# Four row tiles of the seventh sequence in the input's buffers, its routing drawn together, and the first experts' work half a step earlier

## The chip, the core and the metric

The kernel runs on one core of one Trainium2 chip. The core has five engines that run their own instruction streams and meet at semaphores: TensorE (PE), VectorE (DVE), ScalarE (ACT), GpSimd (POOL) and SyncE (SP), which issues most of the DMA transfers. The metric is the device time of one execution in microseconds (us).

## What is computed

The input is 8 sequences of 2496 rows of 256 numbers. Each is filtered in the frequency domain, and its 19968 result rows go through a mixture of 8 experts, one expert for each row.

```python
X = np.fft.rfft(x, axis=1)                      # x: 8 x 2496 x 256
y = np.fft.irfft(X * (filt_r + 1j * filt_i), n=2496, axis=1)
x = y.reshape(19968, 256)
logits = x @ w_gate                             # 8 experts
expert_idx = np.argmax(logits, axis=1)
gate_w = softmax(logits)[expert_idx]            # of each row
for e in range(8):
    xe = x[expert_idx == e]
    out[expert_idx == e] = gate_w * (np.maximum(xe @ w1[e], 0) @ w2[e])   # 256 -> 1024 -> 256
```

## The kernel before

**Tiling.** The transform of length 2496 is taken as 39 x 64 in two stages of matmuls. A unit u is one sequence b and one half h of the 256 columns, so there are 16 units. The middle of the transform is cut into 80 steps t, five to a unit. A step runs through the engines so: `spec1` transposes on PE (`pt`) and copies on ACT (`z`, line 317); `spec2` multiplies on PE (`px`); `filt_` makes three products with the filter on DVE (`tr`, `ti`, `ti`, lines 345 to 347); `join` adds them (`p`, line 355: POOL for the steps below 71, DVE after that); `spec3` multiplies back on PE (`pi`) and ACT copies the result to memory (`U`, line 371). Below, px77 is the `px` of step 77. The input of a unit comes in tiles `x` from a pool `xp` with 4 buffers under the tag "x" (`loadx`), and `forward1` reads them (`f`).

**A sequence's tail.** When both units of a sequence are in `U`, its routing chain begins, `route1` to `route6`: products with the gate (`plw`, `lw`, `pgl`, `gl`, `pl`), the choice of the expert (`rmx`, `lg`, `eq`, `oh`), ranks inside each expert's block by a product with a triangle (`pp`) and a scan (`sa`, `sb`), and the number of the slot that each row goes to (`dest`, line 623). Beside it the inverse runs over 11 row tiles j of two row groups each: `inv1` transposes (`pg`) and copies on ACT (`gh`, line 639), `inv2` multiplies (`py`) and copies on ACT into a row tile `yt` (line 649; 5 buffers), `inv3` adds the gate's value and the row's number to `yt` (DVE, line 656) and scatters the two row groups to the table `xs` in DRAM by an indirect DMA that POOL issues (line 158): 22 scatters for a sequence.

**The experts.** `weights` closes the pools that the transform no longer needs, the input's `xp` among them, and opens the experts' in the same memory. A block is 128 rows of one expert. `load` reads it (`xb`, line 957, on SP's queue), `loadw` brings an expert's weights in two transfers of about 1 MB (`wa` and `wb`, line 991, SP). `prep` (DVE, lines 1009 to 1018) finds a power-of-two scale, `split` writes the rows as two halves in f16 (`xs`, ACT line 1023 and DVE line 1024), `turn` transposes them by a DMA (`xt`, line 1031, SP). `layer1` (`ph`), the halves `hs`, `hh`, `hl`, `layer2` (`po`) and `out_` (`ot`) follow. The first blocks of the experts hold rows of the first six sequences only, so they can run before the last two are done.

**What sets the order.** No scheduler: each piece is given a number by `at(key, f, ...)`, the pieces are sorted by it and written out, and every engine works through its own instructions in that order, waiting at the head of its queue. The unit of the key is one step; `PLACE[0]` = 80.9 is the key at which the first expert block runs. `RT` holds the places of the ten parts of a routing chain, times a factor `c`.

Of the kernel before, what the change touches and what calls it, by code (L numbers as in the profile page):

```python
# [9 lines left out]
F32 = mybir.dt.float32  # L10
# [17 lines left out]
GP = 3 * N1  # L28
DUP = 18
NPAIR = NG // 2  # L30
ROW = 260
NW = 2
# [81 lines left out]
def tile_fft_moe(ctx, tc, x, filt_r, filt_i, w_gate, w1, w2, cst, out):  # L114
    nc = tc.nc
    B = x.shape[0]
# [9 lines left out]
    for b, m in ((B - 3, 8), (B - 1, 20)):  # L126
        sure = -(-(S * (b + 1) - E * 127) // 128)
        n = min(m, -(-(sure - taken - E) // 2))
# [56 lines left out]
    with ExitStack() as fctx:  # L185
# [5 lines left out]
        wp = pool(name="wp", bufs=2)  # L191
# [8 lines left out]
        xp = early(name="xp", bufs=4)  # L200
# [33 lines left out]
        def loadx(u, c, eng=(nc.sync,) * 3):  # L234
            b, h = divmod(u, 2)
            xv = x[b].rearrange("(n1 n2) d -> n1 n2 d", n2=N2)[
                :, :, h * 128 : (h + 1) * 128
            ]
            g0, g1 = (HEAD if u < 2 else BANKS)[c]
            if u < 2 and c < 2:  # L240
                t = Uf[2 + u][:GP, 128 * g0 : 128 * g1]
                t = t.rearrange("p (g d) -> p g d", d=128)
            else:
                t = xp.tile([GP, 4, 128], F32, name=f"x{u}_{c}", tag="x")
            for l in range(3):
                n = min(g1, NG if l == 0 else NG - 1) - g0
                s0 = 3 * g0 + l
                eng[l].dma_start(
                    t[l * N1 : (l + 1) * N1, :n, :],
                    xv[:, s0 : s0 + 3 * (n - 1) + 1 : 3, :],  # L250
                )
            for g in range(g0, g1):
                xt[u, g] = t[:, g - g0, :]
# [388 lines left out]
        def inv2(b, j):  # L642
            gh = sti.pop((b, j))
            ps = (pY if b < B - 1 else pB).tile(
                [128, 2, D], F32, name=f"py{b}_{j}", tag="pY" if b < B - 1 else "pF"
            )
            nc.tensor.matmul(ps[:GP], lhsT=dm, rhs=gh[:GP], start=True, stop=True)  # L647
            yt = wp.tile([GP, 2, ROW], F32, name=f"yt{b}_{j}", tag="yt", bufs=5)
            nc.scalar.copy(yt[:, :, :D], ps[:GP])
            sti[b, j] = yt  # L650

# [102 lines left out]
        for c in range(3):  # L754
            loadx(0, c)
# [11 lines left out]
        for j in range(6):  # L767
            forward1(0, j)
        loadx(1, 0)
        loadk(bm, "bm", 1, 2)  # L770
        loadf(1, 2)
        loadx(1, 1)
        loadx(1, 2)
        twice(0)
# [29 lines left out]
        def at(key, f, *a):  # L804
            work.append((key, f, a))
# [18 lines left out]
        K = {"s2": 1.394, "sr": 1.65, "si": 1.85, "s3": 3.6, "f": 0.063, "fd": 0.75, "w": 6.0, "wp": 4.1}  # L824
        RT = (0.0, 0.4, 0.45, 0.9, 1.3, 1.7, 2.2, 2.5, 2.9, 3.3)
        slow = lambda t: min(1.0, max(0.6, 1.0 - 0.06 * (t - 72)))
        for t in range(NT):
            u, it = divmod(t, 5)
# [9 lines left out]
            if 0 < u and u + 1 < NU_ALL and it == 0:  # L838
                for j in range(6):

                    n = 6 * (u + 1) + j - 4
# [10 lines left out]
        PLACE = (80.9, 90.5, 110.5)  # L852
        done = []
        for b in range(B):
            rho = slow(10 * b + 9)
            s0 = 10 * b + 9 + K["s3"] * rho + 0.05
            c = 1.0 if b < B - 1 else 0.6
            for i, f in enumerate(
                (
                    (route1, 0),  # L860
                    (route1b, 0),
                    (route1, 1),
                    (route1b, 1),
                    (route2,),
                    (route3,),
                    (route4,),
                    (route4b,),
                    (route5,),
                    (route6,),
                )  # L870
            ):
                at(s0 + c * RT[i], f[0], b, *f[1:])
            lead = 2.0 if b < B - 1 else 1.3


            t = 10 * b + 20
            d = 0.55
            if b < B - 1:
                z = PLACE[0] - 2.75 if b == B - 2 else t + K["s3"] * slow(t) - 0.15
                d = min(0.75, (z - s0 - lead) / (NPAIR - 1))  # L880
            for j in range(NPAIR):
                z = s0 + lead + j * d
                at(z, inv1, b, j)
                at(z + 0.7 * c, inv2, b, j)
                z = max(z + 1.2 * c, s0 + c * RT[9] + 0.1 + 0.9 * d * j)
                for gg in range(2):
                    at(z + 0.45 * d * gg, inv3, b, j, gg)
            if b in [r for r, _, _ in SEG]:
                for s, v in enumerate(SEG):
                    if v[0] == b:  # L890
                        at(s0 + c * RT[9] + 0.2 + 0.1 * s, finish, s)
            done.append(z)
            if b == B - 1:
                at(z + 0.1, tails)
                for e in range(E):
                    at(z + 1.2 + e, tail, e)
        for q in range(2 * E):
            e, i = divmod(q, 2)
            z = K["w"] + K["wp"] * q
# [197 lines left out]
        for s, (r, m, n) in enumerate(SEG):  # L1097
            n *= m
            a = PLACE[s]
            z = PLACE[s + 1] if s + 1 < len(SEG) else a + 0.5 * n  # L1100
# [8 lines left out]
        opened = lambda s: done[SEG[s][0]] + 0.4  # L1109

        def when(k, n):

            s, i, m, b0 = units[k]
            b = b0 + m - 1
            z, d, _ = tau[b]
            if n == 0:
                return z + 0.5 * d
            nx, dx = (tau[b + 1][0], tau[b + 1][1]) if b + 1 < NB else (z + d, d)
            return nx + 0.95 * dx

        at(PLACE[0] - 2.0, weights)
        for k in range(nu):
            s, i, m, b0 = units[k]
            z, d, _ = tau[b0]
            at(max(opened(s), z - 2.0, PLACE[0] - 1.95), load, k)
            for n in range(2):
                at(max(opened(s) + 0.02, when(k - NW, n) + 0.01 if k >= NW else PLACE[0] - 1.9 + 0.7 * (2 * k + n), PLACE[0] - 1.9), loadw, k, n)
        for b in range(NB):
            z, d, s = tau[b]
            y = max(opened(s) + 0.3, z - 1.1)  # L1130
            at(y, prep, b)
            at(y + 0.05, split, b)
            at(y + 0.1, turn, b)
            at(z, layer1, b, 0)
            at(z + 0.2 * d, halves, b, 0)
            at(z + 0.25 * d, layer1, b, 1)
            at(z + 0.45 * d, halves, b, 1)
            nx, dx = (tau[b + 1][0], tau[b + 1][1]) if b + 1 < NB else (z + d, d)
            at(nx + 0.5 * dx, layer2, b, 0)
            at(nx + 0.75 * dx, layer2, b, 1)  # L1140
            at(nx + 0.95 * dx, out_, b)
            at(nx + 0.95 * dx + 0.5, send, b)
# [4 lines left out]
        n = nc.values_load(nblk[0:1, 0:1], min_val=0, max_val=NBLK)  # L1147
# [50 lines left out]
```

## Time and profile before

| | us |
|---|---|
| median of 3 runs | 1410.51 |
| lowest and highest run | 1407.64 and 1411.91 |
| profiled execution, its time | 1408.65 |
| profiled execution, its span | 1406.7 |
| PE busy in the span | 1313.4 (93%) |
| ACT, DVE, POOL busy | 846.1, 834.4, 466.2 |
| mean granted clock of TensorE | 0.988 of full speed |

The span is the time from the first to the last instruction of the profiled execution; 1.95 us lie around it. All times in the text count from the span's start. In a line of the timeline stand the start, the duration, the engine, the line of the code, the operation, what it writes and reads, the number of instructions that were put together, and in brackets how long the engine was idle before it and what released it.

### The profile page before, as it was taken

The numbers are of one execution on the slowest core, as the hardware profiler recorded it, in microseconds if no ns is written. First come the engines' busy times: TensorE is split into PE (matmuls) and PEld (weight loads), VectorE is DVE, ScalarE is ACT, GpSimd is POOL, SyncE is SP. The second block draws the span as 40 slices with busy tenths as digits, with TensorE's granted clock in tenths as the row PEclk, the third lists the DMA queues.
The fourth block names the chain that finished last, engine by engine and source line by source line (L and its number), as shares of the span: only waits on it lengthen the run. The fifth ranks groups of instructions, "written<-read, shape, count | busy, mean of one in ns | idle before, by whom it ended". The sixth has DMA issues, their size and how long they took to land.

```text
span 1406.7 us, 39039 instructions
## 1 busy us (share of the span) xinstructions
PE 1313.4 (93%) x14855; PEld 1175.6 (84%) x14855; DVE 834.4 (59%) x2391; ACT 846.1 (60%) x1444; POOL 466.2 (33%) x446
## 2 busy tenths in 40 slices
PE   6789999989999599899999998999999999999997
PEld 5777777777777477789999987999999999999997
DVE  1688879888796455345555554555555555555552
ACT  3567667766676355455665655665655666666654
POOL 3527476484654513423211111111111111111111
PEclk9999999999999899999999999999999999999999
DMA  9746555564643343496373389337337336336431
GB/s 175 205 139 203 164 190 179 165 194 147 193 129 107 108 114 81 118 272 185 83 192 79 79 240 300 78 74 197 75 75 192 76 77 192 81 76 159 111 74 43
DMA packets 198272, 197.71 MB, mean 141 GB/s; under 512 B 104008, under 2 KB 177339, under 8 KB 189827
## 3 DMA queue, kind: packets, MB, share of 16 engines
q1 hardware_dynamic: 178142, 151.96, 40.0%
q0 software_dynamic: 19472, 42.51, 10.9%
q8 instruction: 118, 1.93, 0.6%
q10 hardware_dynamic: 468, 0.72, 0.2%
q14 instruction: 72, 0.58, 0.1%
HBM read 344.12 MB, written 61.56 MB: 288 GB/s over the span
## 4 chain that ended last, share of the span: by engine, by line
PE 57%; DMA 5%; issue 3%; DVE 2%; ACT 1%; SPq 1%; another core or an unknown queue 1%; POOL 0%; POOLq 0%; ACTq 0%; DVEq 0%
PE ph L1044 27%; PE po L1070 26%; DMA wa<-wscr 3%; PE py L647 1%; PE pg L633 1%; PE px L326 1%; DMA wb<-wscr 1%; DMA xt<-xs 1%; PE pi L366 1%; DMA xs<-yt,dest 0%; POOL out_dram L158 0%; DVE hl L1058 0%; PE f L263 0%; PE plw L497 0%
## 5 line engine op out<-in xcount | busy, mean ns | idle before, releaser
L1044 PE MATMUL ph<-xt,wa 128*128 128x128 f16 x7728 | 463.2, 220 | 18.5 <-DMA wa<-wscr 7.9
L1044 PEld LDWEIGHTS <-wa 128*128 128x128 f16 x7728 | 447.4, 98 | 29.9 <-issue 14.4
L1070 PE MATMUL po<-wb,hh 128*128 128x256 f16 x2576 | 431.2, 273 | 6.1 <-ACT ot L1086 4.3
L1058 DVE TENSOR_TENSOR hl<-hs,hh 128x512 f16<-128x512 f32 x322 | 222.9, 692 | 350.9 <-ACT hh L1052 296.5
L158 POOL DMA_INDIRECT out_dram<-ot,t x161 | 158.2, 982 | 672.8 <-DVE xs L1024 570.2
L1070 PE MATMUL po<-wb,hl 128*128 128x256 f16 x1288 | 351.1, 273 | 0.0
L1070 PEld LDWEIGHTS <-hh 128*128 128x128 f16 x2576 | 245.5, 98 | 36.6 <-issue 8.4
L1050 ACT ACTIVATE hs<-ph 128x512 f32<-128x512 f32 x322 | 191.8, 596 | 104.5 <-PE ph L1044 83.9
L158 POOL DMA_INDIRECT xs<-yt,dest x176 | 185.2, 1052 | 139.5 <-issue 76.3
L1023 ACT ACTIVATE xs<-xb,s 128x256 f16<-128x256 f32 x161 | 82.1, 510 | 226.6 <-DVE s L1013 222.0
L1052 ACT CAST hh<-hs 128x512 f16<-128x512 f32 x322 | 199.5, 620 | 10.3
L1070 PEld LDWEIGHTS <-hl 128*128 128x128 f16 x1288 | 126.1, 98 | 14.8
L371 ACT COPY U<-pi 128x512 f32<-128x512 f32 (+1 forms) x80 | 87.3, 1091 | 59.8 <-PE pi L366 42.2
L355 POOL TENSOR_TENSOR p<-tr,ti 128x512 f32<-128x512 f32 x71 | 91.1, 1283 | 94.6 <-DVE ti L347 79.0
L1024 DVE SCALAR_TENSOR_TENSOR xs<-xb,s,xs 128x256 f16<-128x256 f32 x161 | 78.0, 484 | 59.6 <-ACT xs L1023 58.5
L647 PE MATMUL py<-gh,dm 117*117 117x512 f32 x176 | 93.0, 609 | 12.1 <-issue 9.2
L326 PEld LDWEIGHTS px<-z,bm 128*128 128x128 f32 x640 | 80.9, 195 | 18.7 <-issue 11.4
L366 PE MATMUL pi<-cm,p 128*128 128x128 f32 (+1 forms) x640 | 86.8, 279 | 8.4 <-POOL p L355 6.8
L263 PE MATMUL f<-a,x 117*128 117x117 f32 (+1 forms) x628 | 87.7, 278 | 5.1 <-ACT U L371 1.8
L326 PE MATMUL px<-z,bm 128*128 128x128 f32 x640 | 88.4, 282 | 3.2 <-ACT z L317 1.4
L366 PEld LDWEIGHTS pi<-cm,p 128*128 128x128 f32 x640 | 78.8, 193 | 12.2 <-POOL p L355 7.2
L345 DVE TENSOR_TENSOR tr<-px,ff 128x512 f32<-128x512 f32 x80 | 54.8, 685 | 57.6 <-PE px L326 25.9
(171 smaller groups left out, 1339.6 us busy)
## 6 DMA issues: line engine op xcount, KB each, us to landing
wb<-wscr SPq DMA_DIRECT2D x133, 1040.0 KB
wa<-wscr SPq DMA_DIRECT2D x133, 1024.0 KB
xb<-xs SPq DMA_DIRECT2D x161, 130.0 KB
wf<-in_moe_w_dram SPq DMA_DIRECT2D x32, 512.0 KB
x<-in_x_dram SPq DMA_DIRECT2D x210, 78.0 KB
wscr<-wh SPq DMA_DIRECT2D x8, 1040.0 KB
wscr<-wh SPq DMA_DIRECT2D x8, 1024.0 KB
xs<-yt,dest POOLq DMA_INDIRECT x176
```

The source lines that it names most:

```text
L158: nc.gpsimd.indirect_dma_start(out=dst, out_offset=bass.IndirectOffsetOnAxis(ap=idx, axis=0), in_=src, in_offset=None, bounds_check=bound, ...
L263: nc.tensor.matmul(ps[:, n : n + m], lhsT=xt.pop((u, g))[:m], rhs=a1[:m, :m], start=True, stop=True,)
L326: nc.tensor.matmul(ps[:, kk], lhsT=bm[:, 4 * it + kk], rhs=z[:, kk], start=True, stop=True,)
L355: e.tensor_tensor(p, tr, ti, op=ALU.add)
L366: nc.tensor.matmul(ps[:, o : o + n], lhsT=p[:, kk], rhs=cm[:, k, :n], start=True, stop=True)
L371: nc.scalar.copy(U[u % NU].rearrange("p n r -> p r n")[:, r0 : r0 + o // 64, :], ps[:, :o].rearrange("p (r n) -> p r n", n=N2),)
L647: nc.tensor.matmul(ps[:GP], lhsT=dm, rhs=gh[:GP], start=True, stop=True)
L1044: nc.tensor.matmul(ps[:, f], lhsT=w[:, p : p + 128], rhs=xt[:, r, c], start=(n == 0), stop=(n == 5))
L1050: nc.scalar.activation(s, ps, AF.Relu, scale=1.0 / B23)
L1052: nc.scalar.copy(hh, s)
L1058: nc.vector.tensor_tensor(hl, s, hh, op=ALU.subtract)
L1070: nc.tensor.matmul(ps, lhsT=h2[q][:, f % 4], rhs=wv[:, r, f], start=(f == 0 and n == 0), stop=(f == 7 and n == 2),)
```

## The change

The 7th of the 8 sequences is b = 6, in the code `B - 2`. For it alone:

1. The tiles under the tag "x" get the size of a row tile pair, and row tiles 5 to 8 of the sequence take buffers of that tag, where the input's tiles were, so that its 11 row tiles have 9 buffers in place of 5.
2. Its routing chain's places are multiplied by 0.75 (before 1.0), and the key at which its inverse has to be through is 0.55 of a step earlier.
3. `weights`, the first loads of blocks and weights, and the first block's `prep`, `split` and `turn` stand 0.5 to 0.85 of a step earlier.

```diff
@@ loadx
-                t = xp.tile([GP, 4, 128], F32, name=f"x{u}_{c}", tag="x")
+                t = xp.tile([GP, 2 * ROW], F32, name=f"x{u}_{c}", tag="x")
+                t = t[:, 0:512].rearrange("p (g d) -> p g d", d=128)
@@ inv2
-            yt = wp.tile([GP, 2, ROW], F32, name=f"yt{b}_{j}", tag="yt", bufs=5)
+            if b == B - 2 and j % 9 > 4:
+                yt = xp.tile([GP, 2 * ROW], F32, name=f"yt{b}_{j}", tag="x")
+                yt = yt.rearrange("p (g d) -> p g d", d=ROW)
+            else:
+                yt = wp.tile([GP, 2, ROW], F32, name=f"yt{b}_{j}", tag="yt", bufs=5)
@@ the routing chain's and the inverse's keys
-            c = 1.0 if b < B - 1 else 0.6
+            c = {B - 1: 0.6, B - 2: 0.75}.get(b, 1.0)
-                z = PLACE[0] - 2.75 if b == B - 2 else t + K["s3"] * slow(t) - 0.15
+                z = PLACE[0] - 3.3 if b == B - 2 else t + K["s3"] * slow(t) - 0.15
@@ the experts' keys
-        at(PLACE[0] - 2.0, weights)
+        at(PLACE[0] - 2.5, weights)
-            at(max(opened(s), z - 2.0, PLACE[0] - 1.95), load, k)
+            at(max(opened(s), z - 2.0, PLACE[0] - 2.45), load, k)
...
-            y = max(opened(s) + 0.3, z - 1.1)
+            y = max(opened(s) + 0.3, z - (1.1 if b else 1.95))
```

The line between, for `loadw`, has its two -1.9 replaced by -2.4. The number of instructions is the same on every engine; POOL's order is the same too. The other engines' orders differ only from the routing of the 7th sequence to the first blocks of the experts. (Line numbers of the changed kernel are 1 higher up to line 648 and 5 higher from there.)

On PE, in the routing: `pl` is the logits' product, `pp` the ranks' product, `pt` is of step 74, `px` of 73, `pi` of 71. Before:

```order
L538 MATMUL pl_5055<-gl_4996,dm 117x176
L311 MATMUL pt_5063<-ident,T_110 128x128 x4
L326 MATMUL px_5070<-z_4994,bm 128x128 x4
L366 MATMUL pi_5089<-cm,p_4980 128x128 x4
L633 MATMUL pg_0_5095<-ident,U_122 117x128
...
L574 MATMUL pp_5104<-oh_5077,ltri 117x176
```

After:

```order
L539 MATMUL pl_5041<-gl_4989,dm 117x176
L264 MATMUL f_15_5_5057<-a_112,x_5_4863 128x117
L264 MATMUL f_15_5_5057<-a_112,x_5_4863 128x39
L312 MATMUL pt_5072<-ident,T_110 128x128 x4
...
L575 MATMUL pp_5079<-oh_5065,ltri 117x176
...
L327 MATMUL px_5082<-z_5012,bm 128x128 x4
L367 MATMUL pi_5097<-cm,p_4980 128x128 x4
```

`px`, `pi` and `pg_0` moved from ahead of `pp` to behind it, and the last piece of `f` from ahead of `pl` to between the two.

On PE, from the last but one row tile's product to the first expert matmul `ph`; the `pi` are those of steps 76 to 78 before, and of 75 to 78 after. Before:

```order
L647 MATMUL py_9_5388<-gh_9_5336,dm 117x512
L366 MATMUL pi_5396<-cm,p_5304 128x128 x4
L647 MATMUL py_10_5405<-gh_10_5372,dm 117x512
L326 MATMUL px_5409<-z_5358,bm 128x128 x4
L311 MATMUL pt_5441<-ident,T_111 128x128 x4
L366 MATMUL pi_5476<-cm,p_5379 128x128 x4
L326 MATMUL px_5496<-z_5446,bm 128x128 x4
L366 MATMUL pi_5519<-cm,p_5467 128x128 x4
L1044 LDWEIGHTS wa_5430
L1044 MATMUL ph_0_5549<-xt_5503,wa_5430 128x128
```

After:

```order
L648 MATMUL py_9_5363<-gh_9_5334,dm 117x512
L367 MATMUL pi_5371<-cm,p_5261 128x64
L367 MATMUL pi_5371<-cm,p_5261 128x128 x3
L327 MATMUL px_5377<-z_5293,bm 128x128 x4
L312 MATMUL pt_5382<-ident,T_111 128x128 x4
L648 MATMUL py_10_5392<-gh_10_5354,dm 117x512
L367 MATMUL pi_5444<-cm,p_5340 128x128 x4
L327 MATMUL px_5450<-z_5387,bm 128x128 x4
L312 MATMUL pt_5475<-ident,T_111 128x128 x4
L367 MATMUL pi_5494<-cm,p_5405 128x128 x4
L327 MATMUL px_5500<-z_5480,bm 128x128 x4
L367 MATMUL pi_5526<-cm,p_5491 128x128 x4
```

pi75, px77 and pt78 stood ahead of `py_9` before and stand behind it after, so `py_9` and the row tiles ahead of it moved forward.

On SP, the experts' first transfers, with the reads of table entries between them left out. Before:

```order
L957 DMA xb_5437<-xs 128x260
...
L991 DMA wa_5430<-wscr 128x4096
...
L991 DMA wb_5431<-wscr 128x4160
L1031 DMA_TRANSPOSE xt_5503<-xs_5489 128x4x128
...
L957 DMA xb_5513<-xs 128x260
```

After:

```order
L962 DMA xb_5458<-xs 128x260
...
L1036 DMA_TRANSPOSE xt_5484<-xs_5468 128x4x128
...
L996 DMA wb_5427<-wscr 128x4160
...
L996 DMA wa_5428<-wscr 128x4096
...
L962 DMA xb_5520<-xs 128x260
```

The first `wa` now stands ahead of the first `xb`; the first `wb` and the second expert's `wa` stand behind the first transpose `xt`, and the third and fourth blocks' `xb` behind both.

On DVE the first block's `prep` and its part of `split` stand ahead of the filter blocks of steps 78 and 79 (before: between the two), and `dest` stands two filter blocks behind the choice of the expert's first instruction `rmx` (before also two, and one more between `gl` and `rmx`). On ACT the first block's `xs` stands behind `z` of step 79 and ahead of `U` of steps 77 and 78 (before: behind `U` of step 77).

More of the change, by code (lines that the diff above doesn't have):

```diff
@@ L1124, in tile_fft_moe @@
             z, d, _ = tau[b0]
-            at(max(opened(s), z - 2.0, PLACE[0] - 1.95), load, k)
+            at(max(opened(s), z - 2.0, PLACE[0] - 2.45), load, k)
             for n in range(2):
-                at(max(opened(s) + 0.02, when(k - NW, n) + 0.01 if k >= NW else PLACE[0] - 1.9 + 0.7 * (2 * k + n), PLACE[0] - 1.9), loadw, k, n)
+                at(max(opened(s) + 0.02, when(k - NW, n) + 0.01 if k >= NW else PLACE[0] - 2.4 + 0.7 * (2 * k + n), PLACE[0] - 2.4), loadw, k, n)
         for b in range(NB):
             z, d, s = tau[b]
-            y = max(opened(s) + 0.3, z - 1.1)
+            y = max(opened(s) + 0.3, z - (1.1 if b else 1.95))
             at(y, prep, b)
```

## The prediction

> **What bounds the kernel now.** I read the page first, then the windows, then the timelines of the stretch that the change touches.
>
> ```profile
> span 1406.7 us, 39039 instructions
> PE 57%; DMA 5%; issue 3%; DVE 2%; ACT 1%; SPq 1%; another core or an unknown queue 1%; POOL 0%; POOLq 0%; ACTq 0%; DVEq 0%
> ```
>
> PE carries most of the chain that ends last. What matters is where it is not full. The windows give from, to, length, then the busy time of PE first, and the granted clock, DMA share and GB/s last.
>
> ```profile
> 464.00:468.00 4.00, 4.00 (x26) 2.71 (x24) 0.00 (x0) 1.20 (x3) 3.08 (x4) 1.00 0.34 103
> 472.00:476.00 4.00, 0.00 (x0) 0.00 (x0) 2.44 (x7) 0.84 (x2) 2.32 (x3) 0.57 0.24 78
> 476.00:480.00 4.00, 0.69 (x1) 0.47 (x2) 0.00 (x0) 1.41 (x3) 3.08 (x4) 0.50 0.30 91
> 496.00:500.00 4.00, 2.94 (x35) 2.12 (x36) 1.78 (x3) 2.85 (x5) 0.00 (x0) 0.95 1.12 380
> 500.00:540.00 40.00, 37.20 (x447) 31.48 (x440) 26.18 (x124) 21.01 (x41) 7.12 (x7) 1.00 0.26 68
> 600.00:620.00 20.00, 17.17 (x234) 15.83 (x232) 10.64 (x39) 11.07 (x22) 5.05 (x5) 1.00 0.86 252
> 620.00:640.00 20.00, 20.00 (x269) 18.68 (x267) 10.46 (x35) 12.34 (x23) 6.18 (x6) 1.00 1.09 313
> ```
>
> PE is full up to 468, nearly empty to 480, and full again from 620. So the change works on the one large hole in the middle, the handover from the transform to the experts, and since PE has no slack after 620, a first expert matmul that starts x earlier ends the kernel x earlier, if the last sequence's chain between 500 and 620 moves along. It should: it begins behind that first block. PE on both sides of the hole:
>
> ```profile
> 441.30 0.53 PE L538 MATMUL pl<-gl,dm 117*117 117x176 f32 x2
> 445.81 0.29 PE L574 MATMUL pp<-oh,ltri 117*117 117x176 bf16 x1 [1.32 <-DVE oh L565]
> 465.37 0.60 PE L311 MATMUL pt<-ident,T 128*128 128x128 f32 x4
> 467.15 1.02 PE L647 MATMUL py<-gh,dm 117*117 117x512 f32 x2
> 468.92 1.16 PE L366 MATMUL pi<-cm,p 128*128 128x128 f32 x8 [0.74 <-issue]
> 479.31 2.06 PE L647 MATMUL py<-gh,dm 117*117 117x512 f32 x2 [9.24 <-issue]
> 485.68 1.16 PE L326 MATMUL px<-z,bm 128*128 128x128 f32 x8 [1.36 <-ACT z L317]
> 487.40 1.13 PE L366 MATMUL pi<-cm,p 128*128 128x128 f32 x8 [0.56 <-DVE yt L656]
> 492.58 4.47 PE L1044 MATMUL ph<-xt,wa 128*128 128x128 f16 x48 [4.05 <-DMA xt<-xs]
> 503.55 2.85 PE L1044 MATMUL ph<-xt,wa 128*128 128x128 f16 x48
> ```
>
> PE waits 0.74 + 9.24 + 1.36 + 0.56 + 4.05 = 15.95 us between 468 and 492.58. The 9.24 are py_10's, which needs gh_10. ACT, DVE, POOL and SP say why:
>
> ```profile
> 465.49 0.59 ACT L649 COPY yt<-py 117x512 f32<-117x512 f32 x1 [1.74 <-DMA xs<-yt,dest]
> 473.59 0.59 ACT L317 COPY z<-pt 128x512 f32<-128x512 f32 x1 [4.72 <-remote]
> 475.74 0.59 ACT L649 COPY yt<-py 117x512 f32<-117x512 f32 x1 [1.57 <-remote]
> 478.68 0.59 ACT L639 COPY gh<-pg 117x512 f32<-117x512 f32 x1 [2.35 <-remote]
> 479.16 0.59 ACT L649 COPY yt<-py 117x512 f32<-117x512 f32 x1
> 483.62 1.10 ACT L371 COPY U<-pi 128x512 f32<-128x512 f32 x1 [3.87 <-PE pt L311]
> 488.07 0.51 ACT L1023 ACTIVATE xs<-xb,s 128x256 f16<-128x256 f32 x1 [1.42 <-DVE s L1013]
> 498.24 0.51 ACT L1023 ACTIVATE xs<-xb,s 128x256 f16<-128x256 f32 x1
> 498.65 1.08 ACT L371 COPY U<-pi 128x512 f32<-128x512 f32 x1
> 441.07 0.68 DVE L345 TENSOR_TENSOR tr<-px,ff 128x512 f32<-128x512 f32 x1
> 443.80 0.33 DVE L547 TENSOR_REDUCE rmx<-pl 117x22 f32<-117x176 f32 x1
> 454.34 0.18 DVE L623 TENSOR_TENSOR dest<-df,dup 117x22 int32<-117x22 f32 x1
> 471.45 0.69 DVE L345 TENSOR_TENSOR tr<-px,ff 128x512 f32<-128x512 f32 x1 [8.58 <-PE pi L366]
> 487.17 0.17 DVE L656 COPY yt<-meta 117x8 f32<-117x8 f32 x1
> 455.44 0.99 POOL L158 DMA_INDIRECT xs<-yt,dest  x1 [15.12 <-issue]
> 481.67 0.99 POOL L158 DMA_INDIRECT xs<-yt,dest  x1 [0.30 <-issue]
> 479.08 0.33 SPq L991 DMA_DIRECT2D wb<-wscr  x1
> 489.12 1.31 SPq L1031 DMA_TRANSPOSE xt<-xs  x1
> 491.16 0.90 SPq L957 DMA_DIRECT2D xb<-xs  x2
> ```
>
> The striking thing is z78 at 473.59. Its `pt` began at 465.37 and took 0.60, so its result was there at 465.97, and ACT waited 4.72 us for "remote", a releaser that the profile does not name. The next two results of PE, py_8 and pg_10, were used at 475.74 and 478.68, both long after PE had left them. So in this stretch PE's results are taken up late, one after another, about (478.68 - 471.45) / 3 = 2.41 us apart, while POOL issues scatters back to back. I can't say from the trace why; how much of it remains is the main unknown of this prediction.
>
> **The change part by part.**
>
> *Four more buffers (5 to 9 for 11 row tiles).* Before, yt_5 and later ones waited for the scatters of yt_0 and later. Now only yt_9 and yt_10 reuse a buffer, whose scatters are some ten us older. That takes away ACT's waits like the 1.74 at yt_7 (465.49), which sat under PE's full stretch: nothing by itself. What it adds: the experts' memory now lies over buffers that yt_5 to yt_8 hold until their scatters land. The first tiles behind that wait, `hh` and `hl` of block 0, need yt_7's, the 15th and 16th scatter. At (481.67 - 455.44) / 19 = 1.38 us or less each, the 16th is issued by about 454.4 + 15 x 1.38 = 475.1; with a few us to land that is before the first `ph` of any case below but the quickest. I take 0.
>
> *The routing chain drawn together.* One filter block (443.80 - 441.07 = 2.73 us) leaves the path from `gl` to `rmx`, and `pl` itself comes one `px` and a wait earlier, by my reading at about 439.65. Then `rmx`, `lg`, a block, `eq` to `oh`: `pp` at about 445.0. Before it was 445.81, but PE had done px, pi and pg_0 ahead of it. What these take at PE's full pitch stands in the chain of waits:
>
> ```profile
> 452.80 0.44 PE pg L633 x4
> 453.24 0.89 PE px L326 x8
> ```
>
> A `pi` has the shape of a `px`, a `pt` that of a `pg`, so the three are 0.89 + 0.89 + 0.44 = 2.2 us. So PE's full stretch loses 2.2 - 0.8 = 1.4 us at `pp`: the one cost in this part that nothing covers. `dest` comes some 3 us earlier, at about 451.5, but yt_0's copy of `meta` now stands behind step 74's tr, ti, ti, and I put the first scatter at 454.4 against 455.44, so 1 us earlier. Nothing waits on PE for that. The last of the 22 would be issued at 454.4 + 21 x 1.30 = 481.7.
>
> *Row tiles ahead of pi75, px77, pt78.* py_9 ended at 467.15 + 1.02 = 468.17. Now 1.4 later for `pp`, and 2.2 earlier, since pi75, px77 and pt78 (0.89 + 0.89 + 0.44) stand behind it: 467.4. pt78 then ends at about 469.6 instead of 465.97. What this buys: gh_10 no longer stands behind z78 and yt_8 on ACT, so py_10 doesn't keep PE waiting for two late results.
>
> *Preparation and xs ahead.* Before, from DVE's end of yt_10's copy (487.17, behind p77) to `ph` lay 492.58 - 487.17 = 5.41 us. That tail remains, but it moves ahead of the filter blocks of steps 78 and 79 and, on ACT, right behind z79. It saves the waits for pi77 and U77, which before lay between 483.62 and 488.07 (4.45 us).
>
> *SP's queue.* `xt0` no longer stands behind `wb0`, which waited until 479.08 for the last read of `U`; `xt0` was issued at 489.12, so that wait hid nothing and its removal gives 0. On the other side xb2 and xb3 now queue behind wb0 and wa1, 2.1 MB. At the 380 GB/s of the window from 496, when weights were moving, that is 5.5 us; at the 103 of the window from 464, 20 us. In the likeliest case wb0 goes out at about 482.7, so xb2 lands by 488 to 503, and `xs` of block 2, which stands ahead of U79 on ACT, needs it 498.24 - 492.58 = 5.7 us after `ph` starts, at about 492. The cost is between 0 and 11; the row from 496 is the one with the same transfers in flight, so I take 0 and keep the rest for the range. [...]
>
> *The sum.* Five late results of PE stand on the way from py_9 to the first block's `xs`: px77, pt78, py_10, pi76, pt79 (ACT takes U76 and z79 in order ahead of xs0). I start at the first late one of before, 471.45, and keep the pitch of 2.41: the fifth is taken at 471.45 + 4 x 2.41 = 481.1. z79 takes 0.59, xs0 starts at 481.7, and from xs0 to `ph` it is 492.58 - 488.07 = 4.5: `ph` at 486.2, 6.4 us earlier. Against the profiled execution's 1408.65 that is 1402.3, against the median, which is 1.86 higher, 1404.1. I say 1403.
>
> **The rivals.**
>
> *The lateness goes away (a larger gain).* With results taken up at once, px77 ends at 469.3, DVE's three products, yt_9's copy and p77 end at 472.2, and 5.4 us later `ph` starts: 477.7, 14.9 earlier. Then `ph` also would not run slowly: its first 48 matmuls took 4.47 us where the next 48 took 2.85, so 1.6 more. Less what xb2 may cost, 12 to 16 earlier: 1393 to 1398. For it: the row tiles now leave in a steady stream and ACT's queue has no head that waits for buffers. Against: the scatters are as dense as before. [...]
>
> *The head start is used up (no change).* `ph` starts some 5 us earlier, but xb2's 0 to 11 us hold U79 and with it the last sequence's routing, on which the stretch from 500 to 620 hangs, or that stretch's idle time (2.80 us from 500 to 540, 2.83 from 600 to 620) grows by as much. For it: U79 began at 498.65 directly behind `xs` of block 2 (498.24), so that there is no slack between the two. Against: the 380 GB/s. That gives 1407 to 1412.
>
> *More results late (slower).* The pitch applies not to the five results on the path but to each one in the burst. In the new order pg_10, py_9, pi75 and px78 stand between them in PE's order, all read by ACT or DVE. Nine results from 471.45 on put the last at 471.45 + 8 x 2.41 = 490.7, xs0 at 491.3 and `ph` at 495.8, 3.2 later than before: 1412 to 1414, some us more with xb2. It decides from the eighth result on (xs0 was at 488.07: (488.07 - 0.59 - 471.45) / 2.41 = 6.7 pitches). For it: the same dense scatters, without the pauses of before, so with no place to catch up. Against: yt_9 at 479.16 came 0.48 behind gh_10, so not each result pays.
>
> **How the numbers follow.** A measurement of this kernel tells about 0.3%, 4.2 us, from no change; against the median that means faster below 1406.3 and slower above 1414.7. Forecast, `ph` 4 to 9 us earlier: 0.40, own range 1399 to 1406. Lateness gone, 1393 to 1398: 0.24. Used up: 0.23. More late, or xb2 at its worst, 0.13; about half of it is over 1414.7, and some of the used-up cases go there too. So faster 0.64, same 0.24, slower 0.12. The range leaves out the lowest twentieth and the slower side's end: 1393 to 1412.
>
> **What would show it.** Right: the first `ph` between 483 and 489; z79 and xs0 next to each other on ACT; PE's wait ahead of `pp` about 3 to 4 us instead of 1.32; py_9 ending within 1 us of before; no wait over 1 us for a scatter on `hh` or `hl` of block 0; U79 between 491 and 494; PE full from about 613. Wrong: results of PE taken up at once (then 1395), xs of block 2 waiting for xb2 (then no gain), or ACT waits for "remote" that reach past 488 (then slower).

## The result and the profile after

The changed kernel is slower: 1416.66 us median against 1408.03 for the kernel before on the same chip, a ratio of 1.0054 (95% interval 1.0044 to 1.0065), or 7.6 us. The forecast was 1403, faster. The changed kernel's profiled execution took 1417.81 us, its span was 1415.9.

PE around the handover, from the changed kernel's timeline:

```profile
443.09 0.40 PE L575 MATMUL pp<-oh,ltri 117*117 117x176 bf16 x1 [3.52 <-DVE oh L566]
443.43 1.98 PE L327 MATMUL px<-z,bm 128*128 128x128 f32 x8
445.21 1.92 PE L367 MATMUL pi<-cm,p 128*128 128x128 f32 x8
463.26 1.12 PE L648 MATMUL py<-gh,dm 117*117 117x512 f32 x2 [2.45 <-issue]
475.31 1.03 PE L648 MATMUL py<-gh,dm 117*117 117x512 f32 x2
481.05 0.60 PE L312 MATMUL pt<-ident,T 128*128 128x128 f32 x4
489.47 2.08 PE L327 MATMUL px<-z,bm 128*128 128x128 f32 x8 [6.93 <-ACT z L318]
495.06 4.83 PE L1049 MATMUL ph<-xt,wa 128*128 128x128 f16 x48
503.72 0.80 PE L498 MATMUL plw<-U,wg 128*32 128x351 f32 x8 [2.15 <-ACT U L372]
508.67 3.21 PE L1049 MATMUL ph<-xt,wa 128*128 128x128 f16 x48
```

The first `ph` starts at 495.06 (before 492.58, forecast 486.2). The great wait has not gone but moved: before it was 9.24 us at py_10, now it is 6.93 at px79. A second cost stands at `pp`: PE waits 3.52 us and then runs px and pi at half speed (1.98 and 1.92 us, with a pitch of 1.78 and 1.70, in place of 0.89). The second `ph` has lost more than the first, 508.67 against 503.55. Of the 9.2 us by which the span is longer, 2.5 have built up by the first `ph` and 5.1 by the second; the rest comes later, and no experiment takes it apart.

The other engines there, from the same kernel:

```profile
450.52 0.18 DVE L624 TENSOR_TENSOR dest<-df,dup 117x22 int32<-117x22 f32 x1
471.33 0.69 DVE L346 TENSOR_TENSOR tr<-px,ff 128x512 f32<-128x512 f32 x1 [10.93 <-remote]
488.83 0.59 ACT L318 COPY z<-pt 128x512 f32<-128x512 f32 x1 [5.40 <-remote]
489.32 0.51 ACT L1028 ACTIVATE xs<-xb,s 128x256 f16<-128x256 f32 x1
501.34 0.42 DVE L1014 TENSOR_REDUCE m<-xb 128x1 f32<-128x257 f32 x1 [3.76 <-DMA xb<-xs]
502.58 1.08 ACT L372 COPY U<-pi 128x512 f32<-128x512 f32 x1
453.94 0.99 POOL L158 DMA_INDIRECT xs<-yt,dest  x1 [13.35 <-ACT gh L640]
468.21 1.00 POOL L158 DMA_INDIRECT xs<-yt,dest  x1 [0.30 <-issue]
474.47 0.99 POOL L158 DMA_INDIRECT xs<-yt,dest  x1 [5.26 <-ACT gh L640]
486.12 1.00 POOL L158 DMA_INDIRECT xs<-yt,dest  x1 [0.31 <-issue]
```

Put the POOL rows beside the two "remote" waits. PE's results are late from some 6 us after POOL's first scatter, all are there at 471.3, 2 us after POOL paused (469.2), nothing is late from 474 to 481, and z79, whose `pt` ended at 481.65, is taken at 488.83, 1.7 us after POOL's last scatter ended (487.12). In the kernel before, the same had happened at 483.6, 0.95 us after its sixth scatter of the second run. So in these two traces lateness sets in some 6 us into an unbroken run of scatters, and what is still held when the run ends is let go 1 to 2 us behind it. Some results are let through singly inside a run, as the four of the kernel before between 471.45 and 478.68; what decides that isn't shown.

The same shows further on in the kernel before, where the 8th sequence's scatters and the outputs' make two runs of six, one from 568.78 to 576.43. PE, from the timeline of before:

```profile
573.89 0.44 PE L1044 MATMUL ph<-xt,wa 128*128 128x128 f16 x5
574.75 0.22 PE L1044 MATMUL ph<-xt,wa 128*128 128x128 f16 x1 [0.41 <-issue]
575.47 0.22 PE L1044 MATMUL ph<-xt,wa 128*128 128x128 f16 x1 [0.51 <-issue]
576.22 0.22 PE L1044 MATMUL ph<-xt,wa 128*128 128x128 f16 x1 [0.53 <-issue]
577.63 3.80 PE L1044 MATMUL ph<-xt,wa 128*128 128x128 f16 x40 [1.19 <-issue]
```

From 5.5 us after the run's start PE, waiting for nothing that the profile names, gets out one matmul in about 0.7 us, and it goes on at full pace 1.2 us after the run has ended. So it is not only that its results are seen late.

To compare kernels, lateness is worked out thus: the trace has the moments at which PE's semaphore rises; from each I subtract the end of PE's last finished instruction that raises it, and take the largest difference within a run of scatters and the 1.5 us behind it. A run is unbroken where less than 0.7 us lies between two; the outputs' indirect DMAs count with the scatters.

### The profile page after: what moved, and what is told of

Its sections match the earlier page's. It is cut to its first block, busy times and chain, and to the rows that moved or that the text cites. A ratio compares the mean times of both kernels' runs of the same rounds, so it can differ in the third digit from the quotient of the medians.

```text
span 1415.9 us, 39040 instructions
## 1 busy us (share of the span) xinstructions
PE 1321.5 (93%) x14855; PEld 1181.1 (83%) x14855; DVE 833.4 (59%) x2391; ACT 846.5 (60%) x1444; POOL 465.4 (33%) x446
## 4 chain that ended last, share of the span: by engine, by line
PE 47%; DMA 5%; issue 2%; DVE 1%; SPq 1%; ACT 1%; POOL 0%; POOLq 0%
PE ph L1049 24%; PE po L1075 23%; DMA wa<-wscr 2%; DMA wb<-wscr 2%; DVE hl L1063 0%; POOL out_dram L158 0%; DMA xt<-xs 0%; DMA xb<-xs 0%; SPq L1036 0%; SPq L948 0%; DVE m L1014 0%; ACT hh L1057 0%; ACT hs L1055 0%; ACT xs L1028 0%; DVE xs L1029 0%
```

## The experiments

Theory A: unbroken runs of scatters on GpSimd make PE's results late. Theory B: the data of the scatters, or the order of the work, does. Theory C: the drawn-together routing costs at `pp`. Theory D: the loads behind 2.1 MB of weights cost.

**Pauses in the changed kernel.**

```diff
+        pad = fp.tile([128, 256], F32, name="pad")      # and a memset
...
             scatter(xs[:, :], dest[:, g : g + 1], yt[:, gg], ...)
+            if b == B - 2 and g % 3 == 2:
+                for _ in range(2):
+                    nc.gpsimd.tensor_tensor(pad, pad, pad, op=ALU.mult)
```

> The changed kernel with two small GpSimd multiplies on a scratch tile (some 1.5 us together) behind every third scatter of the 7th sequence; nothing else differs. Theory A: PE's completions are taken up late only while GpSimd issues more than about four scatters in one unbroken run (in both traces, runs of 1 to 4 have at most 1.45 us of lateness, runs of 6 and more 3.5 to 8.6). Then the lateness between 455 and 490 is gone, although GpSimd is busier than before, and the first expert matmul starts at 478 to 482 instead of 495.06; the time falls by 12 to 17 us against the changed kernel, to about 1400 to 1405 (the kernel before: 1408). Theory B: the lateness comes with the scatters' data or with the order of the work on ACT and PE, not with the run's length. Then the same 22 scatters only take longer, the first expert matmul stays at 493 to 500, and the time stays at 1415 to 1420.

Measured: 1406.3 us, ratio to the kernel before 0.9986 (0.9972 to 0.9999), so about 10 us below the changed kernel. No result over 1.2 us late until 560. PE, ACT and POOL of this kernel:

```profile
481.87 4.47 PE L1054 MATMUL ph<-xt,wa 128*128 128x128 f16 x48
493.86 1.40 PE L500 MATMUL plw<-U,wg 128*32 128x351 f32 x8 [5.85 <-ACT U L374]
476.51 0.58 ACT L320 COPY z<-pt 128x512 f32<-128x512 f32 x1 [0.64 <-PE pt L314]
491.80 0.62 ACT L1062 CAST hh<-hs 128x512 f16<-128x512 f32 x1 [4.25 <-DMA xs<-yt,dest]
459.33 0.99 POOL L158 DMA_INDIRECT xs<-yt,dest  x1 [0.30 <-issue]
460.34 1.31 POOL L671 TENSOR_TENSOR pad<-pad 128x256 f32<-128x256 f32 x2
461.83 1.03 POOL L158 DMA_INDIRECT xs<-yt,dest  x1 [0.18 <-issue]
```

z79 is taken 0.64 us after its wait begins, not 5.40, and `ph` starts 13.2 us earlier, as theory A said, although the same 22 scatters are issued and POOL is busier than before. That speaks against B; how fast the scatters' data come is settled below, with the runs of five. The time gained less than `ph`, and two rows say why: `hh` waits 4.25 us for the landing of scatters out of the input's buffers, which the pauses made later, and with it ACT's U79 and the second half of `plw` are late.

**The same pauses in the kernel before.** The same edit there.

> The kernel before with the same two GpSimd multiplies behind every third scatter of the 7th sequence. Theory A: the runs of 14 and 6 scatters are broken up, py_10 no longer waits 9.24 us, the first expert matmul starts at 480 to 484 instead of 492.58, and the time falls by 8 to 12 us to about 1397 to 1400. Theory B: no gain, 1407 to 1411, or some us slower, since the row tiles' buffers come free later.

Measured: 1402.26 us, 0.9949 (0.993 to 0.9968): 7.2 us faster. The first `ph` starts at 483.72, and no result is over 1.6 us late until 560. With pauses in both, the kernel without the change is the faster by 4 us.

**The routing's factor back.** `c = 1.0 if b < B - 1 else 0.6` in the changed kernel.

> The changed kernel with the routing chain's factor back at 1.0 (buffers, the inverse's earlier end and the experts' earlier work stay). Theory C: the drawn-together chain costs, because PE waits 3.52 us at the ranks' product and then runs at half clock to 448 (about 2.8 us more). Then the wait at pp is under 1.5 us, the granted clock between 440 and 448 is 1.00, and the time is 3 to 6 us below the changed kernel, 1411 to 1414. Theory A alone: the run of scatters only starts a few us later and ends later, so the first expert matmul comes at 495 or after it and the time is that of the changed kernel or more, 1416 to 1420.

Measured: 1410.92 us, 1.0021 (1.0007 to 1.0034). A third of a per cent, 4.6 us by the ratios, is given back. The wait at `pp` is 1.32 us again, and the clock from 440 to 448 is 1.00 where the changed kernel had 0.57:

```profile
440.00:448.00 8.00, 6.68 (x55) 5.98 (x54) 7.56 (x19) 4.66 (x10) 0.00 (x0) 1.00 0.50 164
443.73 0.29 PE L575 MATMUL pp<-oh,ltri 117*117 117x176 bf16 x1 [1.32 <-DVE oh L566]
```

The same row of the changed kernel:

```profile
440.00:448.00 8.00, 4.91 (x24) 4.91 (x25) 6.12 (x15) 1.15 (x2) 0.58 (x2) 0.57 0.59 184
```

So the wait comes with the factor. But the factor does more than draw the routing together: the keys of the row tiles' products and scatters hold it too (`at(z + 0.7 * c, inv2, b, j)`). With it back at 1.0, PE's last results of the transform fall differently against POOL's runs:

```profile
479.28 0.59 ACT L318 COPY z<-pt 128x512 f32<-128x512 f32 x1 [0.27 <-PE pt L312]
484.64 3.14 PE L1049 MATMUL ph<-xt,wa 128*128 128x128 f16 x48
493.44 0.42 DVE L1014 TENSOR_REDUCE m<-xb 128x1 f32<-128x257 f32 x1 [5.42 <-DMA xb<-xs]
495.83 1.40 PE L498 MATMUL plw<-U,wg 128*32 128x351 f32 x8 [6.37 <-ACT U L372]
```

The second run of scatters is unbroken here too (eight, from 474.82 to 485.68), but `pt79` ends 4.4 us after its start, before lateness sets in, and not 7.2 us after it as in the changed kernel. z79 waits 0.27 us and the first `ph` starts 10.4 us earlier. Most of that is lost again, since the third block waits 5.42 us for `xb`. So the run shows what the factor costs in all; that the wait at `pp` is the whole of it, as C says, is not shown.

**The four buffers alone**, in the kernel before.

> The kernel before with the four more row-tile buffers alone. Theory A: the run of scatters has one cause fewer to pause (in the kernel before the pause at 473.8 came from a row tile that was late), so it is at least as long and ends at about 484; the first expert matmul stays at 490 to 496 and the time within 4 us of the kernel before, 1405 to 1412. If the buffers were what was short: first expert matmul 5 us earlier, 1403.

Measured: 1405.28 us, 0.9986 (0.9971 to 1.0001), the first `ph` at 487.84. Not slower, and perhaps 2 us faster; the first `ph` came earlier than expected, in a profile of the fastest of the ten executions (1402.49). The run is unbroken for 14 and then 8 scatters, so the buffers don't remove the lateness.

**The weights' keys back.** Both `PLACE[0] - 2.4` of `loadw` back to `- 1.9` in the changed kernel.

> The changed kernel with the weights' transfers alone back at their old keys, so that on SP the second expert's wa again stands behind the third and fourth blocks' xb (wb0 still ahead of them). Theory D: part of the loss is that xb2 lands behind 2.1 MB of weights (in the changed kernel the third block's prep waited 3.76 us for it at 501.34, and U79 stood behind that block's xs on ACT). Then that wait falls under 1 us, the second half of plw comes 1 to 2 us earlier against the first ph, and the time falls by 1 to 4 us against the changed kernel, to 1412 to 1415. If theory D is wrong (U79 waits for something else) the time stays at 1415 to 1418. The lateness of the runs of scatters is untouched in both.

Measured: 1411.62 us, 1.0023 (1.0012 to 1.0034): 4.4 us given back. The third block's preparation waits 0.34 us for `xb` in place of 3.76, and the second half of `plw` starts 1.86 us after the first (in the changed kernel 2.95):

```profile
497.37 0.80 PE L498 MATMUL plw<-U,wg 128*32 128x351 f32 x8
499.23 0.80 PE L498 MATMUL plw<-U,wg 128*32 128x351 f32 x8 [1.06 <-ACT U L372]
```

D's wait is there, and the gain is above what was expected. The wait explains 1.1 us of the 4.4; the first `ph` is earlier too in this profile, at 491.68, since z79 was let through at 485.45, 1.2 us before the run of scatters ended. Why isn't shown, and the profile is of the fastest execution (1406.33).

**Both back.** The two edits before this together.

> The changed kernel with two parts undone together, the routing's factor (back at 1.0) and the weights' keys (back at the old ones); no pauses. If theories C and D are the whole of the loss and add up, each having given back about 0.3%, the time is 0.998 to 1.001 of the kernel before, 1405 to 1410, and what is left (buffers, the inverse's earlier end, the earlier preparation) is worth about nothing as long as the run of scatters is unbroken. If the two undo the same microseconds: 1.002 as with either alone, 1411.

Measured: 1405.51 us, 0.9992 (0.9977 to 1.0008). The two add up to the whole loss: 1.0054 - 0.0033 - 0.0031 = 0.9990. These ratios come from different chips, and the changed kernel's own was 1.0039 to 1.0063 (last experiment), so each part alone is uncertain by about 0.1%; that both together take the loss back is measured in one run. What is left of the change, buffers, earlier inverse and earlier preparation, is worth nothing measurable while the run of scatters is unbroken; the first `ph` is at 488.81 there, 3.8 us earlier than before.

**Pauses in the 8th sequence too**, in the kernel before: the multiplies also for `b == B - 1 and g % 2 == 1`.

> The kernel before with the two multiplies behind every third scatter of the 7th sequence, as in the run before it, and also behind every second scatter of the 8th. Theory A: the two unbroken runs of six indirect DMAs near 563 and 576, each with 3.8 us of lateness and single matmuls issued 0.7 us apart, are gone too, and the time falls by another 3 to 7 us, to 1395 to 1399. If the runs of six cost nothing there (PE has other waits in that stretch): 1401 to 1404, as with the 7th sequence alone.

Measured: 1392.55 us, 0.9881 (0.9858 to 0.9903), faster by 16.8 us, more than expected. The four executions lie between 1390.1 and 1401.38, and the profile is of the slowest. Its window from 560 to 580 has PE busy for 20.00 us of 20, before 17.36.

```profile
560.00:580.00 20.00, 20.00 (x238) 17.40 (x236) 8.91 (x34) 13.10 (x26) 15.25 (x19) 1.00 0.43 105
```

**Buffers and short pauses**: the kernel before with the four buffers, one multiply behind every fourth scatter of the 7th sequence, and the 8th's pauses.

> The kernel before with the four more buffers, one single multiply (some 0.9 us with its gaps) behind every fourth scatter of the 7th sequence, and the pauses in the 8th. Theory A with a pause of 0.9 us being enough: no lateness over 1.5 us from 455 to 490, ACT no longer waits up to 4.63 us for a row tile's buffer (as with five buffers and pauses), the first ph at 477 to 481, time 1392 to 1397. If 0.9 us is too short to drain: lateness of 2 to 5 us stays in the burst, first ph at 484 to 490, time 1398 to 1403.

Measured: 1394.88 us, 0.9894 (0.9873 to 0.9914). The first `ph` at 479.83, from 455 nothing is over 0.3 us late until 487, then 1.43 and 2.87 once each, so pauses of one multiply did not keep it under the expected 1.5.

**The change with its costs taken out**: routing's factor and weights' keys back, short pauses, the 8th's pauses.

> The changed kernel with each cost found so far taken out: the routing factor back at 1.0, the weights' transfers back at their old keys, a multiply behind every fourth scatter of the 7th sequence, pauses in the 8th. Theories A, C and D together: no wait over 1.5 us at pp, no lateness over 1.5 us, no wait for xb2; first ph at 474 to 480 and the time at 1388 to 1396, below the kernel before with the same pauses. If the earlier preparation and inverse are worth nothing by themselves: 1395 to 1399, the same as that one.

Measured: 1395.65 us, 0.9903 (0.9883 to 0.9923), the first `ph` at 478.19. That is where the forecast's rival without lateness put it (477.7), and yet the time is no better than that of the kernel before with pauses. The gain at the first `ph` is given back at once. First this kernel, then the kernel before with pauses in both sequences:

```profile
478.19 3.56 PE L1054 MATMUL ph<-xt,wa 128*128 128x128 f16 x48
486.14 0.60 ACT L1060 ACTIVATE hs<-ph 128x512 f32<-128x512 f32 x1 [2.51 <-remote]
488.84 0.80 PE L500 MATMUL plw<-U,wg 128*32 128x351 f32 x8 [3.79 <-ACT U L374]
```

```profile
482.92 2.84 PE L1049 MATMUL ph<-xt,wa 128*128 128x128 f16 x48 [1.55 <-DMA xt<-xs]
490.22 0.80 PE L499 MATMUL plw<-U,wg 128*32 128x351 f32 x8 [2.38 <-ACT U L373]
```

Of the 4.7 us at the first `ph` 1.4 are left at the second half of `plw`. U79 stands behind the first block's two `hs` on ACT, and the second `hs` came with the last scatters, when PE's results were once more 3.36 us late: a pause of one multiply was too short here.

**How long a run may be.** Pauses behind every fifth scatter, `g % 5 == 4`, in the kernel before.

> The kernel before with the two multiplies behind every fifth scatter of the 7th sequence instead of every third. Runs of 1 to 4 had at most 1.6 us of lateness with py and z in them, runs of 6 had 3.8. Theory A with a threshold near 5.5 us from the run's start (where PE's single matmuls began to be issued 0.7 us apart in the runs of 6): five scatters end 6.2 us after the run's start, so each run shows 0.5 to 2 us of lateness and the time lies between, 1401 to 1406. If the lateness came from the total of scatters in 30 us and not from the unbroken run: lateness of 4 us or more returns and the time is 1405 to 1409.

Measured: 1400.32 us, 0.996 (0.9948 to 0.9973), the first `ph` at 482.94. The four runs of five have at most 0.27 us of lateness, less than expected, and the two runs of six in the 8th sequence 3.95 and 3.74. The 22 scatters took about as long as in the kernel before (454.21 to 488.50 against 455.44 to 490.46), so it is not how fast they come that matters, but the run without a break. With that B falls. Here is the lateness by runs over the kernels of this study on the chips that have it; not each run of six shows it (the first expectation had put them all at 3.5 or more), probably since it is seen only when PE finishes something within the run:

```
unbroken scatters   runs   largest lateness, us
1 to 3              3439   3.4 (five over 1.6)
4                     24   1.45
5                      6   0.27
6                     29   9.9 (18 of them 3.5 to 4.2, nine under 2)
8 to 14               17   6.5 (all but two over 1.3)
```

**Real work as the pause.** In the kernel before, the joins of steps 71 to 77 stay on GpSimd: `t < 78` in place of `t < 71`.

> The kernel before with the join of steps 71 to 77 left on GpSimd (1.29 us each, as in the earlier steps) in place of VectorE, so that real work stands between the scatters of the 7th sequence where the other kernels have a scratch multiply. Theory A, on a chip with the lateness: the runs are cut to six and fewer, lateness under 4 us, the first ph at 484 to 490, 1400 to 1407. Against it: a join queues behind two scatters on GpSimd (2.6 us) and is 0.6 us longer than on VectorE, which delays each step's pi; if that weighs more, 1408 to 1414. On a chip without the lateness only this delay is left: 2 to 6 us slower than the kernel before there.

Measured: 1401.91 us, 0.9948 (0.9931 to 0.9965), as much as the scratch multiplies give in that sequence. The first `ph` at 482.87. One run of eight scatters is left, behind the last join, with 1.77 us of lateness. The edit also takes the joins off VectorE, which the scratch multiplies don't.

**Shorter pauses**: one multiply behind every fifth scatter of the 7th and every second of the 8th sequence, in the kernel before.

> The kernel before with one single multiply (some 0.9 us from scatter to scatter more) behind every fifth scatter of the 7th sequence and behind every second of the 8th. Theory A with both findings so far (a run of five has no lateness, a pause of 0.9 us is enough after four): no lateness over 1.6 us anywhere from 455 to 600, row tiles' buffers come free earlier than with longer pauses, 1388 to 1393, the same as or some us below the run with pauses behind every third scatter (1392.55). If 0.9 us does not empty what a run of five has filled: lateness of 2 to 4 us in the later runs of the burst, 1393 to 1400.

Measured: 1385.05 us, but the kernel before took 1383.06 on this chip: 1.0018 (1.0004 to 1.0031). In this trace no result of PE was over 0.05 us late up to the program's end; on the other chips even single scatters have up to 0.8, and once 3.1. So the run can't tell whether short pauses are enough; behind every fourth scatter, in the two kernels above, they were not.

**The changed kernel and the kernel before once more**, to see whether the lateness belongs to the chip.

> The changed kernel as it is, once more, on whichever chip this falls to. On the chip of the run with short pauses no result of PE was taken up more than 0.05 us late in any run of scatters, and the kernel before took 1383 us there, 25 us less than on the other chips. If this chip is such a one: no lateness, the first ph at 478 to 482 (theories C and D still cost: the wait at pp and the wait for xb2), and a time within 0.996 to 1.004 of the kernel before. If it is one of the others: lateness of 3 to 6 us in runs of ten and more, first ph at 490 to 496, ratio 1.004 to 1.007 as first measured.

> The kernel before as it is, one profiled look on the same chip. Without the lateness: no result taken up over 0.3 us late although the runs of 14 and 6 scatters are unbroken, py_10 waits under 2 us, first ph at 478 to 483, time 1380 to 1387. With it: first ph at 490 to 494 and 1404 to 1412, as in the first profile.

> The changed kernel once more, on whichever chip this falls to. On a chip without the lateness: first ph at 478 to 482, time within 0.996 to 1.004 of the kernel before there (about 1383). On one with it: ratio 1.003 to 1.007, as measured twice.

Measured: 1414.8 us, 1.0039 (1.002 to 1.0059), and on yet another chip 1417.4, 1.0063 (1.004 to 1.0085). The kernel before took 1412.73 in its one execution there, with py_10 waiting 9.17 us and the first `ph` at 492.30. Both chips have the lateness. In the first of the changed kernel's two traces here z79 was taken at 487.34, 2.8 us before POOL's run ended. So five chips that can be told apart have it. The sixth showed none in its one trace, which is of a kernel with pauses (longest run: six); the kernel before was only timed there, and was 25 us faster than on the others, so that the lateness is missing there without pauses too is likely, not shown. What the change is worth on that chip was not measured.

## Why the prediction was wrong

**The step that failed is the pitch.** The sum took five results of PE (px77, pt78, py_10, pi76, pt79) to be late one after another, 2.41 us apart from 471.45 on, and had z79 taken at 481.1. It was taken at 488.83, and none of the five kept the pitch:

```profile
477.07 1.06 PE L327 MATMUL px<-z,bm 128*128 128x128 f32 x8
477.97 0.60 PE L312 MATMUL pt<-ident,T 128*128 128x128 f32 x4
478.40 1.02 PE L648 MATMUL py<-gh,dm 117*117 117x512 f32 x2
479.27 1.05 PE L367 MATMUL pi<-cm,p 128*128 128x128 f32 x8
478.17 0.69 DVE L346 TENSOR_TENSOR tr<-px,ff 128x512 f32<-128x512 f32 x1 [3.79 <-PE pi L367]
478.61 0.59 ACT L318 COPY z<-pt 128x512 f32<-128x512 f32 x1 [0.34 <-issue]
479.47 0.59 ACT L654 COPY yt<-py 117x512 f32<-117x512 f32 x1 [0.27 <-issue]
482.33 1.10 ACT L372 COPY U<-pi 128x512 f32<-128x512 f32 x1 [2.28 <-issue]
```

px77, pt78 and py_10 were taken up 0.04 us after their ends, pi76 2.0 us after its end, and pt79 alone, which ended at 481.65, 7.2 us after. In place of five equal delays there were two stretches of lateness, one in each of POOL's runs. The first held results from 462.5 to 471.4, of row tiles that the forecast had on time, and let the last five go within 0.3 us. So py_9 ended at 476.34, where 467.4 was forecast and "within 1 us of before" was a sign of being right. The second held pt79's result, and with it z79. I had written that POOL issued scatters back to back meanwhile, and did not make that the clock of the sum. Here z79 was let go 1.7 us behind the end of the second run, which was forecast at 481.7 + 1 and measured at 487.1. From z79 to `ph` it then took 6.2 us in place of 5.1, with px79 and pi78 at half speed ahead of `ph`. The forecast's sign of being slower, ACT's waits for "remote" reaching past 488, came true.

**The scatters themselves.** The first was forecast for 454.4 and came at 453.94; `dest` for 451.5, came at 450.52. That the run would be unbroken was wrong: the lateness held up a row tile, POOL paused 5.26 us, and the second run of ten began at 474.47 and lay over px78, pt79 and z79.

**The wait at `pp`** was forecast as 3 to 4 us in place of 1.32, and is 3.52. Its price of 1.4 us left out what follows: the clock at 0.57, px, pi and two pg in 4.9 us instead of 2.7. With that the price of the wait would have been about 3.6. Undoing the factor gave back 4.6, but moved z79 as well, so the two can't be set equal. Slow matmuls stood in the forecast for `ph` alone. In this trace they follow a shorter wait too: behind one of 2.24 us (with one of 1.41 us shortly before) a pg takes 1.14 us in place of 0.60, and the clock from 472 to 476 is 0.58:

```profile
471.82 1.14 PE L634 MATMUL pg<-ident,U 128*117 128x128 f32 x4 [2.24 <-ACT z L318]
472.00:476.00 4.00, 4.00 (x12) 2.62 (x13) 2.32 (x7) 3.18 (x6) 1.23 (x2) 0.58 0.01 2
```

**xb2 behind the weights** was taken at 0, with up to 11 kept for the range. From the issue of wb0 (492.34) to the `xb` behind the weights (501.34) it took 9.0 us where 5.5 were forecast, against 5.7 of cover, and the second half of `plw` came 1.1 us later. Undoing it gave back 4.4 (0.31%), more than the wait that the row shows; z79 was let through earlier there too, and where the rest sits stays open.

**The rivals.** "More results late" gave the right `ph` (495.8 forecast, 495.06 measured) for the wrong reason, the pitch: that is luck. It also left out what follows from the factor and from the weights' keys, whose undoing takes the loss back. "The lateness goes away" has the right mechanism once it is made to go away (478.19 against 477.7), but its 12 to 16 us don't reach the end of the kernel. That `ph` would then run at full pace, 1.6 us in that sum, was my estimate: the first 48 took 3.56 us in that run, and 4.47 as before in the changed kernel with pauses. The 1395.65 us of that run owe about 0.7% to the eighth sequence's pauses (0.9949 and 0.9881 without and with them), and behind the first `ph` the last sequence's routing waits for U79.

## What to carry to other kernels

Look for the releaser that the profile can't name: where several engines wait for "remote" at once and all are let go together, look for an engine whose activity begins and ends with it, before pricing the waits one by one. On the chips where it occurs, cut runs of indirect DMAs after five at most (six such runs were seen here, with 0.27 us at most), with real work of that engine if there is some. Before drawing a chain together, look at what PE did meanwhile: here 3.52 us of idle time were followed by 2.2 us of slow work, and nothing waited for the earlier `dest`. And when a factor is undone in an experiment, look at which other keys hold it.

## What was not expected of the hardware

On five of the six chips an unbroken run of GpSimd's indirect DMAs (0.99 us each, 0.30 between) slowed PE: single matmuls came 0.7 us apart from 5.5 us on, in the 8th sequence of the kernel before, and semaphore rises up to 9.9 us late over all the kernels, while those of ACT and VectorE came within 0.01 us in the two kernels' first traces. With a pause of some 1.5 us after three or five scatters (two multiplies), or after three to six (a join), no result in the seventh sequence's runs was over 1.6 us late; the eight scatters that no join broke had 1.77. Pauses of 0.8 us after four left up to 3.36; breaks of 0.5 to 0.6 us did not help, in the second trace of the kernel before, and neither did the 1.37 us behind a run of 14 in the first. One chip of six didn't show it in its one trace. The cause stays open. Each time in this document comes with a span and a granted clock from trace records, so no run shows how the kernels fare without them.
